# The sign of decoded float64 weights through a Prelu scaling, with the scaling back spread over three engines

## The chip, the cores and the metric

The kernel runs on one core of one Trainium2 chip. The metric is the device time of one execution in microseconds (us), as the median of several runs. Engines go by the profile's names: PE (TensorE matmul), PEld (its weight loads), DVE (VectorE), ACT (ScalarE), POOL (GpSimd), SP (the queue that issues the DMAs).

## The reference, cut to what matters

```python
# q, k, v: (8, 8, 576, 64); chunks of 64 along the sequence
attn = softmax((q_c @ k_c.T) / 8)            # per chunk
x = (attn @ v_c)  ->  (4608 tokens, 512)
h = x @ moe_w_in                             # 512 -> 2048
x = (h * sigmoid(h)) @ moe_w_out             # 2048 -> 512
h = x @ moe2_w_in                            # 512 -> 1024
s = h * softmax(h)
ln = (s - mean(s)) / sqrt(var(s) + 1e-6) * g_ln
out = ln @ moe2_w_out                        # 1024 -> 512
```

The four weight matrices reach the chip as float64, that is, as pairs of 32-bit words; the kernel makes float16 pairs (a high half and a low half that carry the value together) from them on the chip.

## The kernel before

The 4608 tokens are worked on in NB = 9 blocks of 512. For each block the kernel does the attention of four tiles of 128 tokens (`a_scores`, `a_norm`, `a_pv`; block 0 has a simpler form, `f_scores`, `f_norm`, `f_pv`), then the first layer in 16 groups (`h_group`, line 362 and on: twelve matmuls into one bank of PSUM, a Silu on ACT at L366, and `g_split`), then `x_part` (L645 to 647), which gives the input of the second MoE, and, one block later, that second MoE (`m_h`, `m_norm`, `m_out`). Blocks 0 and 1 (FAST = 2) use plain products; blocks 2 to 8 use a scheme with seven products in place of eight, whose combined weights are made during block 1 by `w1_sums` and `w2_sums` (L391 to L406) and written to DRAM.

Every value that enters a matmul is split by `split`: the high half is a float16 copy (L110 on ACT), the low half the value minus the high half (L114 on POOL, L115 on DVE).

**The decoding.** `wq` lists 48 tiles of weights, 128 x 512 float64 each: tiles 0 to 15 for w1, 16 to 31 for w2, 32 to 39 for w3 (names `w3q`), 40 to 47 for w4. `fetch` (L856 in the profile) starts the transfer of one into `wst`, a tile of pairs of int32 words. Three steps follow.

- `dec_scale` (`d1`): L129, ACT takes the upper word as a float32 and multiplies it by 2^-111, which brings the exponent into place. For tiles 0 to 31 the result is in PSUM (`wp`), for 32 to 47 in SBUF (`wy`).
- `dec_bits` (`d2`): three operations on DVE: L136 shifts left by 3, L137 takes in the top three bits of the lower word, and L139 takes the sign out of the upper word and puts it into bit 31.
- `dec_split` (`d3`): tiles 0 to 39 have the high half on ACT (L110) and the low half on POOL (L114); tiles 40 to 47 have their gain (`gs`, from g_ln) taken in, and the low half on DVE (L115).

`weights(n)` does the split of the oldest tile, the scaling of the next, and the bits of the one between; the lists NW0, NX, NW1 and NX1 say how often it is called at each step of blocks 0 and 1. The order on each engine is made by a scheduler from this program order with priorities (`tc.high_priority`); each engine then takes its instructions strictly in that order. The decoded value `wy` lives in tiles of the pools: from tile 28 on (`ytile`) all of them share two buffers (tag "o"), so that the scaling of a tile there needs the release by POOL, or DVE, of the tile two before it.

Attention tiles after block 0 have this chain: maximum (L215), difference (L224), Exp on ACT (L225) or in eight pieces (L222), sum (L226), factors (L231, L233), normalisation (L234, two SBUF operands on DVE), high half (L236 or a DVE copy), low half (L237, on POOL during block 0), a transposing DMA (pT, L239), and the matmuls with v (L256 to L258), whose halves vbh and vbl are made by `prep_v`.

Of the kernel before, what the change touches and what calls it, by code (L numbers as in the profile page):

```python
# [8 lines left out]
F32 = mybir.dt.float32  # L9
F16 = mybir.dt.float16  # L10
I32 = mybir.dt.int32
AF = mybir.ActivationFunctionType
ALU = mybir.AluOpType
# [3 lines left out]
P = 128  # L17
# [8 lines left out]
KD = DM // P  # L26
# [13 lines left out]
S_X2 = 2.0 ** 12  # L40
S_LN = 2.0 ** 10

LEAST = -3.4028234663852886e38


@with_exitstack
def fused(ctx: ExitStack, tc: tile.TileContext, qkv, w1, w2, w3, w4, g_ln, out):
    nc = tc.nc
    V, A, G, T = nc.vector, nc.scalar, nc.gpsimd, nc.tensor
# [19 lines left out]
    PHA = [4, 5, 6, 7, 8, 10, 11, 15, 32, 33, 34, 35]  # L69
    QF = 14  # L70
    DEFER = 7

    const = ctx.enter_context(tc.tile_pool(name="const", bufs=1))
    one = ctx.enter_context(tc.tile_pool(name="one", bufs=1))
# [9 lines left out]
    for d in range(KD):  # L84
        for f in range(4):
            if f % 2 == 0:
                tag = f"w2_{2 * d + f // 2}" if d < 3 else f"q{12 + f // 2}"
                y = one.tile([P, 2, 2, 4, P], F16, tag=tag, name="w2t")
# [8 lines left out]
    gs = const.tile([P, K2], F32, name="gs")  # L97
    mhalf = const.tile([P, 1], F32, name="mhalf")
    zero = const.tile([P, 1], F32, name="zero")


    qb = [const.tile([P, NS, P], F16, name=n) for n in ("qbh", "qbl")]
# [4 lines left out]
    def split(dst_h, dst_l, src, scale, eng_h, eng_l):  # L107

        if eng_h is A:
            A.activation(dst_h, src, AF.Copy, scale=scale)  # L110
        else:
            V.tensor_scalar(out=dst_h, in0=src, scalar1=scale, scalar2=None, op0=ALU.mult)
        if eng_l is G and scale == 1.0:
            return G.tensor_tensor(out=dst_l, in0=src, in1=dst_h, op=ALU.subtract).ins  # L114
        return V.scalar_tensor_tensor(out=dst_l, in0=src, scalar=scale, in1=dst_h,  # L115
                                      op0=ALU.mult, op1=ALU.subtract).ins
# [7 lines left out]
    def dec_scale(c):  # L124
        st, y, wh, wl, gain = c
        if c[1] is None:
            c[1] = ps1.tile([P, 512], I32, tag="mm", name="wp")
        p = c[1]
        A.activation(p.bitcast(F32), st[:, :, 1].bitcast(F32), AF.Copy, scale=2.0 ** -111)  # L129

    def dec_bits(c, y):
        st, p, wh, wl, gain = c
        c[1] = y
        if y is None:
            c[1] = y = p
        V.tensor_scalar(out=p, in0=p, scalar1=3, scalar2=None, op0=ALU.logical_shift_left)  # L136
        V.scalar_tensor_tensor(out=p, in0=st[:, :, 0], scalar=29, in1=p,  # L137
                               op0=ALU.logical_shift_right, op1=ALU.bitwise_or)
        V.scalar_tensor_tensor(out=y, in0=st[:, :, 1], scalar=-2 ** 31, in1=p,  # L139
                               op0=ALU.bitwise_and, op1=ALU.bitwise_or)  # L140

    def dec_split(c):
        st, y, wh, wl, gain = c
        yf = y.bitcast(F32)
        if len(wh.shape) == 3:
            yf = yf.rearrange("p (a b) -> p a b", a=wh.shape[1])
        if gain is None:
            split(wh, wl, yf, 1.0, A, G)
        else:
            split(wh, wl, yf, gain, A, V)  # L150


    ns = [0]
# [215 lines left out]
    def g_split(b, f, eng_h=V):  # L369
        return split(*g_of(b, f), graw.pop(f), S_G, eng_h, V)  # L370
# [318 lines left out]
    def m_fast(b, c, alt=False):  # L689
# [29 lines left out]
        def add(n, out, p, own=True):  # L719
# [3 lines left out]
                out=out, in0=p, in1=out if own else zero.to_broadcast([P, 512]), scale=1.0,  # L723
                scalar=LEAST if first else part[:, i:i + 1], op0=ALU.add, op1=ALU.max,
                accum_out=(part if first else m)[:, i:i + 1])
# [9 lines left out]
        elif not more_(b):  # L735
            uT_tags = ["q10", "q11"]
        m_norm(b, [2 * c, 2 * c + 1], [[(e[i], slice(0, F2))] for i in range(2)], m, e, u_tags, uT_tags,
               G if alt else UL, DEFER if c and more_(b) else 0)

# [90 lines left out]
    warm = const.tile([P, 1], F32, name="warm")  # L830
    G.memset(mhalf, -0.5)
    G.memset(zero, 0.0)
    ident = one.tile([P, P], F32, tag="h2", name="ident")
    make_identity(nc, ident)
    ident16 = const.tile([P, P], F16, name="ident16")
# [7 lines left out]
    for k in range(KD):  # L843
        for n in range(2):
            y = w3q[n, k // 2]
# [23 lines left out]
    def d1():  # L869
        if raw:  # L870
            i, st = raw.pop(0)
            c = [st, None if i < SB else ytile(i), *wq[i][1:]]
            dec_scale(c)
            mid.append((i, c))

    def d2():
        if mid:
            i, c = mid.pop(0)
            dec_bits(c, ytile(i) if i < SB else None)
            out_.append((i, c))  # L880
            if at[0] < 36 or len(raw) + len(mid) < 2:
                fetch()

    def d3():
        if out_:
            i, c = out_.pop(0)
            dec_split(c)

    def weights(n=1):
        for _ in range(n):  # L890
            d3()
            d1()
            d2()

    for x in FIRST:
# [6 lines left out]
        else:  # L902
            t = len(vs0)
            vs0.append(one.tile([P, 512], F32, tag=("vs", "xb0", "xb1", "xb2")[t], name=f"vs0_{t}"))
            nc.sync.dma_start(out=vs0[t], in_=qkv[t, :, 2])
    nc.sync.dma_start(out=gs, in_=g_ln)


    def first(i, what):
# [8 lines left out]
    for x in START.split():  # L918
        if x[0] in "snp":
            first(int(x[1]), x[0])  # L920
        else:
            {"d1": d1, "d2": d2, "d3": d3, "w": weights}[x]()
# [7 lines left out]
    for b in range(NB):  # L930
# [4 lines left out]
        for f in range(K1):  # L935
            if b < FAST:
# [10 lines left out]
                else:  # L947
                    y = g_split(b, f, A)
# [71 lines left out]
    b = NB - 1  # L1020
# [52 lines left out]
```

## Time and profile before

| what | value |
|---|---|
| median of 3 runs | 1180.05 us |
| the runs | 1181.21, 1178.99, 1180.05 us |
| span of the profiled execution | 1179.4 us |
| its own time outside the profile | not recorded apart; the span is 0.65 us below the median |
| PE busy | 1127.8 us (96%) |
| DVE busy | 911.7 us (77%) |
| ACT busy | 802.8 us (68%) |
| POOL busy | 249.1 us (21%) |
| chain that ended last | PE 59%, DVE 16%, ACT 10%, DMA 7%, issue 6%, POOL 2% |

Busy times count instructions that run; an engine that waits is idle. The chain is the work that ended last, followed back from the end of the span. The granted clock is the share of TensorE's full speed in a stretch. Names in rows are written as output<-inputs with buffer numbers left out, and a line can be that of a helper (L110, L114 and L115 stand for every split).

### The profile page before, as it was taken

To read this page: it belongs to the slowest core of one execution; us is meant where nothing else is said; L and a number is where in the kernel's file an instruction comes from. 1 tells how busy PE (TensorE), PEld (TensorE's weight loads), DVE (VectorE), ACT (ScalarE), POOL (GpSimd) and SP (SyncE) were. 2 spreads that over 40 slices of the span, in tenths; PEclk is the share of its full clock that TensorE was granted. 3 is DMA by queue.
4 is the path that set the end of the run, shared out by engine and by line. 5 is a ranking of instruction groups with operands and counts; after the bars stand their busy time and mean duration, and the time that the engine had idled before them with its cause. 6 is when DMAs were issued, how large, how long until landed. Compare 5 with 4: busy or idle time off the path is not lost.

```text
span 1179.4 us, 23566 instructions
## 1 busy us (share of the span) xinstructions
PE 1127.8 (96%) x9036; PEld 769.1 (65%) x9036; DVE 911.7 (77%) x1638; ACT 802.8 (68%) x1475; POOL 249.1 (21%) x243
## 2 busy tenths in 40 slices
PE   5999998998999999999999999999999999999998
PEld 4444443444657875887678767876787677777853
DVE  5999998487578787888778877888689868886453
ACT  6886678676667777856785677568756876577253
POOL 3655433334101510021003100310031002100001
PEclk9999899999999999999999999999999999999999
DMA  7667488543536564776577657666776676665704
GB/s 259 225 190 206 155 233 268 165 135 112 139 113 203 165 189 133 204 204 202 143 192 213 196 151 188 204 198 155 182 211 198 161 180 197 179 161 137 210 21 116
DMA packets 205169, 209.18 MB, mean 177 GB/s; under 512 B 120192, under 2 KB 130432, under 8 KB 205056
## 3 DMA queue, kind: packets, MB, share of 16 engines
q1 hardware_dynamic: 205056, 207.68, 61.5%
q8 instruction: 70, 1.15, 0.4%
q14 instruction: 43, 0.35, 0.1%
HBM read 156.24 MB, written 24.12 MB: 153 GB/s over the span
## 4 chain that ended last, share of the span: by engine, by line
PE 59%; DVE 16%; ACT 10%; DMA 7%; issue 6%; POOL 2%; SPq 0%; ACTq 0%; POOLq 0%; DVEq 0%
PE o_ps L821 5%; PE o_ps L813 5%; PE o_ps L814 5%; PE pa L491 3%; PE pa L594 3%; PE pa L592 3%; PE pa L593 3%; PE pa L493 3%; PE pa L492 3%; DVE vbl L115 2%; PE pa L708 2%; PE pa L709 2%; PE pa L710 2%; PE pb L491 2%; PE pb L493 2%
## 5 line engine op out<-in xcount | busy, mean ns | idle before, releaser
L110 ACT ACTIVATE q<-hc 128x512 f16<-128x512 f32 x196 | 119.1, 624 | 41.4 <-DVE hc L579 16.4
L115 DVE SCALAR_TENSOR_TENSOR q<-hc,q 128x512 f16<-128x512 f32 x196 | 138.0, 719 | 6.9 <-ACT q L110 5.5
L114 POOL TENSOR_TENSOR qbl<-qk,qbh 64x512 f16<-64x512 f32 x54 | 71.0, 1314 | 266.2 <-ACT qbh L110 223.6
L593 PE MATMUL pa<-q,ring 128*128 128x256 f16 x448 | 122.1, 273 | 0.0
L592 PE MATMUL pa<-q,ring 128*128 128x256 f16 x448 | 122.1, 273 | 0.0
L594 PE MATMUL pa<-q,ring 128*128 128x256 f16 x448 | 122.1, 273 | 0.0
L813 PE MATMUL o_ps<-w4h,uT 128*128 128x512 f16 x288 | 109.1, 379 | 0.4 <-DVE e L766 0.4
L814 PE MATMUL o_ps<-w4l,uT 128*128 128x512 f16 x288 | 109.2, 379 | 0.0
L779 POOL TENSOR_TENSOR c<-c,mhalf 128x2 f32<-128x2 f32 (+1 forms) x22 | 14.1, 640 | 392.1 <-DVE c L778 382.2
L492 PEld LDWEIGHTS <-ring 128*128 128x128 f16 x784 | 77.0, 98 | 18.4 <-issue 7.9
L491 PEld LDWEIGHTS <-ring 128*128 128x128 f16 x784 | 77.0, 98 | 11.5 <-DMA ring<-w1s 0.8
L592 PEld LDWEIGHTS <-ring 128*128 128x128 f16 x784 | 76.7, 98 | 11.1
L593 PEld LDWEIGHTS <-ring 128*128 128x128 f16 x784 | 76.7, 98 | 11.0
L493 PEld LDWEIGHTS <-ring 128*128 128x128 f16 x784 | 77.0, 98 | 9.2
L594 PEld LDWEIGHTS <-ring 128*128 128x128 f16 x784 | 76.7, 98 | 8.9
L821 PE MATMUL o_ps<-w4h,uT 128*128 128x512 f16 x288 | 70.2, 379 | 0.0
L491 PE MATMUL pa<-x,ring 128*128 128x256 f16 x224 | 61.6, 275 | 6.7 <-ACT hc L513 4.3
L493 PE MATMUL pa<-x,ring 128*128 128x256 f16 x224 | 61.7, 275 | 0.0
L492 PE MATMUL pa<-x,ring 128*128 128x256 f16 x224 | 61.6, 275 | 0.0
L491 PE MATMUL pb<-x,ring 128*128 128x256 f16 x224 | 61.1, 273 | 0.6 <-DMA ring<-w1s 0.6
L592 PE MATMUL pb<-q,ring 128*128 128x256 f16 x224 | 61.1, 273 | 0.0
L593 PE MATMUL pb<-q,ring 128*128 128x256 f16 x224 | 61.1, 273 | 0.0
(277 smaller groups left out, 3486.4 us busy)
## 6 DMA issues: line engine op xcount, KB each, us to landing
ring<-w1s SPq DMA_DIRECT2D x196, 256.0 KB, 3.4
ring<-w2s SPq DMA_DIRECT2D x196, 256.0 KB, 3.8
wst<-w SPq DMA_DIRECT2D x48, 512.0 KB, 4.1
qk<-qkv SPq DMA_DIRECT2D x29, 512.0 KB, 3.8
vs<-qkv SPq DMA_DIRECT2D x36, 256.0 KB, 3.2
out<-o SPq DMA_DIRECT2D x36, 256.0 KB, 2.2
w1s<-ws SPq DMA_DIRECT2D x32, 128.0 KB, 2.1
w2s<-ws SPq DMA_DIRECT2D x16, 256.0 KB, 2.0
```

What stands on the lines that cost most here:

```text
L110: A.activation(dst_h, src, AF.Copy, scale=scale)
L114: return G.tensor_tensor(out=dst_l, in0=src, in1=dst_h, op=ALU.subtract).ins
L115: return V.scalar_tensor_tensor(out=dst_l, in0=src, scalar=scale, in1=dst_h, op0=ALU.mult, op1=ALU.subtract).ins
L491: T.matmul(ps[:, c], wh, x[:, 0, k], start=first, stop=False, skip_group_check=True)
L492: T.matmul(ps[:, c], wh, x[:, 1, k], start=False, stop=False, skip_group_check=True)
L493: T.matmul(ps[:, c], wl, x[:, 0, k], start=False, stop=k == 1, skip_group_check=True)
L592: T.matmul(ps[:, c], wh, g[:, 0], start=first, stop=False, skip_group_check=True)
L593: T.matmul(ps[:, c], wh, g[:, 1], start=False, stop=False, skip_group_check=True)
L594: T.matmul(ps[:, c], wl, g[:, 0], start=False, stop=q == 1 and f == 3, skip_group_check=True)
L813: T.matmul(ps, uh[:, k], w4h[:, k, :], start=k == 0, stop=False)
L814: T.matmul(ps, uh[:, k], w4l[:, k, :], start=False, stop=False)
L821: T.matmul(ps, ul[:, k], w4h[:, k, :], start=False, stop=k == K2 - 1)
```

## The change

The scaling becomes a Prelu with scale 2^-108 and alpha -2^32: a positive value is multiplied by 2^-108, a negative one by 2^-108 and by -2^32, which makes it positive and sets the bit that the shift by 3 carries into bit 31, the sign. The third bit operation is left out, and the second one now writes `wy`. The decoded value is 2^24 times the weight, so it must be scaled by S_D = 2^-24. For tiles 0 to 39 the string WAYS says who does it: V (13 tiles), DVE subtracts with the scaling in one instruction; G (18 tiles), POOL multiplies by a broadcast constant and then subtracts; A (9 tiles), ACT scales in place and the split is as before. In ways V and G the high half takes the scaling in its own copy. For tiles 40 to 47, `gs` is scaled once on POOL.

```diff
+S_D = 2.0 ** -24
...
+    WAYS = "VG" * 8 + "GAV" * 5 + "G" + "AG" * 4
...
+    down = const.tile([P, 1], F32, name="down")
...
-        A.activation(p.bitcast(F32), st[:, :, 1].bitcast(F32), AF.Copy, scale=2.0 ** -111)
+        A.activation(p.bitcast(F32), st[:, :, 1].bitcast(F32), AF.Prelu, scale=2.0 ** -108, alpha=-2.0 ** 32)
...
         V.tensor_scalar(out=p, in0=p, scalar1=3, scalar2=None, op0=ALU.logical_shift_left)
-        V.scalar_tensor_tensor(out=p, in0=st[:, :, 0], scalar=29, in1=p,
+        V.scalar_tensor_tensor(out=y, in0=st[:, :, 0], scalar=29, in1=p,
                                op0=ALU.logical_shift_right, op1=ALU.bitwise_or)
-        V.scalar_tensor_tensor(out=y, in0=st[:, :, 1], scalar=-2 ** 31, in1=p,
-                               op0=ALU.bitwise_and, op1=ALU.bitwise_or)
-
-    def dec_split(c):
+
+    def dec_split(c, i):
...
-        if gain is None:
-            split(wh, wl, yf, 1.0, A, G)
+        if gain is not None:
+            return split(wh, wl, yf, gain, A, V)
+        way = WAYS[i]
+        if way == "A":
+            A.activation(yf, yf, AF.Copy, scale=S_D)
+            return split(wh, wl, yf, 1.0, A, G)
+        A.activation(wh, yf, AF.Copy, scale=S_D)
+        if way == "G":
+            G.tensor_tensor(out=yf, in0=yf, in1=down.to_broadcast([P, 512]).rearrange("p (a b) -> p a b", a=KD)
+                            if len(yf.shape) == 3 else down.to_broadcast([P, 512]), op=ALU.mult)
+            G.tensor_tensor(out=wl, in0=yf, in1=wh, op=ALU.subtract)
         else:
-            split(wh, wl, yf, gain, A, V)
+            V.scalar_tensor_tensor(out=wl, in0=yf, scalar=S_D, in1=wh, op0=ALU.mult, op1=ALU.subtract)
...
+    G.memset(down, S_D)
...
+    G.tensor_scalar(out=gs, in0=gs, scalar1=S_D, scalar2=None, op0=ALU.mult)
```

The lines of the changed kernel: Prelu L133; shift L140; second bit operation L141; A: scaling L153, then L114 and L118 as before's L110 and L114; G and V: high half L155; G: L157 and L159 on POOL; V: L161 on DVE. Before's L110, L114 and L115 are L114, L118 and L119 there, and later lines are 11 higher (L226 is L237, L234 is L245, L406 is L417).

The scheduler also places the remaining instructions differently. PE's order is the same. Three places:

DVE in block 0, at the normalisation of attention tile 4, the first of block 1 (`ae`; `as` its sums, `g` a split of the first layer). Before:

```order
L139 SCALAR_TENSOR_TENSOR wy_934<-wst_778,wp_835 128x512
L136 TENSOR_SCALAR wp_932<-wp_932 128x512
L136 TENSOR_SCALAR wp_942<-wp_942 128x512
L137 SCALAR_TENSOR_TENSOR wp_932<-wst_821,wp_932 128x512
L226 TENSOR_REDUCE as_909<-ae_908 128x8
L139 SCALAR_TENSOR_TENSOR wy_944<-wst_821,wp_932 128x512
L231 TENSOR_SCALAR as_909<-as_909 128x8
L137 SCALAR_TENSOR_TENSOR wp_942<-wst_831,wp_942 128x512
L233 RECIPROCAL ar_923<-as_909 128x8
L139 SCALAR_TENSOR_TENSOR wy_1034<-wst_831,wp_942 128x512
L234 TENSOR_TENSOR ae_908<-ae_908,ar_923 128x512
```

In the changed kernel (its L226, L235, L237, L245 are before's L215, L224, L226, L234):

```order
L226 TENSOR_REDUCE am_899<-s_ps_874 128x8
L140 TENSOR_SCALAR wp_926<-wp_926 128x512
L119 SCALAR_TENSOR_TENSOR g_852<-h_ps_838,g_852 128x512
L235 TENSOR_TENSOR ae_901<-s_ps_874,am_899 128x512
L141 SCALAR_TENSOR_TENSOR wy_938<-wst_815,wp_926 128x512
L140 TENSOR_SCALAR wp_936<-wp_936 128x512
L141 SCALAR_TENSOR_TENSOR wy_1027<-wst_825,wp_936 128x512
L237 TENSOR_REDUCE as_902<-ae_901 128x8
L242 TENSOR_SCALAR as_902<-as_902 128x8
L244 RECIPROCAL ar_916<-as_902 128x8
L161 SCALAR_TENSOR_TENSOR w2t_90<-wy_938,w2t_90 128x512
L245 TENSOR_TENSOR ae_901<-ae_901,ar_916 128x512
```

Between the sum and the normalisation stood two L139 and one L137; now one L161 stands there.

ACT near the end of block 0, ahead of `vbh`, the high half of v for one of the attention tiles of block 1 (w2t_95 are the last two tiles of w2; `wy`<-`wst` is the scaling of a tile of w3; x2_2 belongs to `x_part`). Before:

```order
L110 ACTIVATE w2t_94<-wy_1368 128x512
L129 ACTIVATE wp_1376<-wst_1221 128x512
L129 ACTIVATE wy_1386<-wst_1362 128x512
L110 ACTIVATE w2t_95<-wy_1378 128x512
L110 ACTIVATE w2t_95<-wy_1388 128x512
L110 ACTIVATE x2_2_1432<-x2_ps_1329 128x512
L110 ACTIVATE vbh_115<-vs_1325 64x8x64 x2
L110 ACTIVATE x_1179<-x_ps_1435 128x4x128
L129 ACTIVATE wy_1396<-wst_1372 128x512
```

In the changed kernel:

```order
L114 ACTIVATE w2t_94<-wy_1359 128x512
L155 ACTIVATE w2t_95<-wy_1369 128x512
L133 ACTIVATE wy_1376<-wst_1352 128x512
L155 ACTIVATE w2t_95<-wy_1378 128x512
L153 ACTIVATE wy_1376<-wy_1376 128x512
L114 ACTIVATE w3q_104<-wy_1376 128x512
L114 ACTIVATE x2_2_1421<-x2_ps_1320 128x512
L133 ACTIVATE wy_1386<-wst_1362 128x512
L114 ACTIVATE vbh_116<-vs_1316 64x8x64 x2
L114 ACTIVATE x_1170<-x_ps_1424 128x4x128
L133 ACTIVATE wy_1393<-wst_1372 128x512
```

The scaling and the high half of the first tile of w3 (wy 1376, L153 and L114) and the scaling of the second (L133, wy 1386) have come to stand before `vbh`.

DVE in block 1, at the last tile of w4 (`w4l`; `c`, `mp`, `e`, `u` belong to the norm of the second MoE); the split of `g` and the lines L403 to L406 of `w1_sums` follow on both sides. Before:

```order
L137 SCALAR_TENSOR_TENSOR wy_2041<-wst_1984,wy_2041 128x512
L139 SCALAR_TENSOR_TENSOR wy_2041<-wst_1984,wy_2041 128x512
L778 SCALAR_TENSOR_TENSOR c_1949<-dv_1946,c_1949 128x1
L670 TENSOR_REDUCE mp_2073<-h2_ps_2046 128x1
L782 TENSOR_SCALAR e_1925<-e_1925,nmu_1944,c_1949 128x1024
L115 SCALAR_TENSOR_TENSOR g_2036<-g_2034,g_2036 128x512
L670 TENSOR_REDUCE mp_2073<-h2_ps_2047 128x1
L115 SCALAR_TENSOR_TENSOR w4l_109<-wy_1979,gs_110,w4h_108 128x512
L784 TENSOR_TENSOR u_1931<-e_1925,u_1931 128x1024
L672 TENSOR_REDUCE mm__2076<-mp_2073 128x1
L115 SCALAR_TENSOR_TENSOR w4l_109<-wy_2041,gs_110,w4h_108 128x512
```

In the changed kernel:

```order
L780 TENSOR_SCALAR nmu_1929<-us_1927 128x1
L789 SCALAR_TENSOR_TENSOR c_1934<-dv_1931,c_1934 128x1
L681 TENSOR_REDUCE mp_2056<-h2_ps_2029 128x1
L793 TENSOR_SCALAR e_1910<-e_1910,nmu_1929,c_1934 128x1024
L119 SCALAR_TENSOR_TENSOR g_2020<-g_2018,g_2020 128x512
L681 TENSOR_REDUCE mp_2056<-h2_ps_2030 128x1
L795 TENSOR_TENSOR u_1916<-e_1910,u_1916 128x1024
L683 TENSOR_REDUCE mm__2059<-mp_2056 128x1
L772 TENSOR_SCALAR nm_2062<-mm__2059 128x1
L119 SCALAR_TENSOR_TENSOR g_2020<-g_2103,g_2020 128x512
```

The two bit operations and both `w4l` of before have left this piece for earlier places.

## Rows read from the trace of the kernel before

**Rows 1.** The page, part 1: busy time of each engine over the whole span.
```profile
PE 1127.8 (96%) x9036; PEld 769.1 (65%) x9036; DVE 911.7 (77%) x1638; ACT 802.8 (68%) x1475; POOL 249.1 (21%) x243
```

**Rows 2.** Busy time by stretch: start:end, length, engines, granted clock, DMA share, GB/s.
```profile
29.50:72.70 43.20, 43.06 (x192) 19.08 (x192) 39.50 (x63) 36.73 (x66) 24.73 (x22) 0.96 0.65 215
72.70:131.20 58.50, 52.53 (x386) 26.15 (x385) 53.63 (x89) 42.67 (x98) 32.39 (x27) 0.91 0.64 192
131.20:197.70 66.50, 60.01 (x294) 28.59 (x293) 62.86 (x115) 53.15 (x95) 24.42 (x24) 1.00 0.77 225
...
94.30:97.70 3.40, 3.40 (x15) 1.24 (x11) 3.23 (x6) 1.67 (x3) 3.39 (x4) 0.50 0.68 214
121.60:128.40 6.80, 6.20 (x36) 3.01 (x37) 6.60 (x9) 3.48 (x6) 2.48 (x2) 0.50 0.60 196
```

**Rows 3.** Waits of PE, 70 to 215 us: total, times, longest, in us.
```profile
PE x_ps L256 <- ACT vbh L110: 2.1, 1, 2.1
PE h_ps L362 <- DVE y L406: 2.1, 1, 2.1
PE x_ps L256 <- DMA pT<-ae: 2.1, 1, 2.1
PE x_ps L258 <- DVE vbl L115: 0.9, 2, 0.6
PE x_ps L645 <- DVE g L115: 0.8, 1, 0.8
PE h_ps L362 <- ACT g L366: 0.8, 1, 0.8
```

**Rows 4.** Groups by line and shape, 0 to 215 us: busy us, mean ns.
```profile
L139 DVE SCALAR_TENSOR_TENSOR wy<-wst,wp 128x512 int32<-128x512 int32 x32 | 21.5, 680 | 1.4 <-POOL w2t L114 1.0
...
L129 ACT ACTIVATE wp<-wst 128x512 f32<-128x512 f32 x32 | 20.3, 637 | 4.4 <-DMA wst<-w 4.3
L114 POOL TENSOR_TENSOR w2t<-wy,w2t 128x512 f16<-128x512 f32 x16 | 19.4, 1215 | 17.5 <-ACT w2t L110 12.1 <-DMA vs<-qkv 5.4
...
L139 DVE SCALAR_TENSOR_TENSOR wy<-wst,wy 128x512 int32<-128x512 int32 x16 | 14.5, 904 | 0.3
...
L129 ACT ACTIVATE wy<-wst 128x512 f32<-128x512 f32 x16 | 10.8, 677 | 11.3 <-POOL w3q L114 6.7 <-DVE w4l L115 3.1 <-POOL w2t L114 1.4
L114 POOL TENSOR_TENSOR w3q<-wy,w3q 128x512 f16<-128x512 f32 x8 | 10.3, 1288 | 15.2 <-ACT w3q L110 15.2
...
L115 DVE SCALAR_TENSOR_TENSOR w4l<-wy,gs,w4h 128x512 f16<-128x512 f32 x8 | 7.4, 933 | 0.0
...
L110 ACT ACTIVATE w3q<-wy 128x512 f16<-128x512 f32 x8 | 5.0, 620 | 1.2 <-DVE wy L139 1.2
```

**Rows 5.** DVE in order of time, 81 to 93 us: start, duration, in us.
```profile
82.53 0.68 DVE L139 SCALAR_TENSOR_TENSOR wy<-wst,wp 128x512 int32<-128x512 int32 x1
...
84.38 0.69 DVE L139 SCALAR_TENSOR_TENSOR wy<-wst,wp 128x512 int32<-128x512 int32 x1
84.99 0.68 DVE L234 TENSOR_TENSOR ae<-ae,ar 128x512 f32<-128x512 f32 x1
...
91.76 1.57 DVE L234 TENSOR_TENSOR ae<-ae,ar 128x512 f32<-128x512 f32 x1
```

**Rows 6.** POOL in order of time, 88 to 94 us.
```profile
88.04 1.15 POOL L237 TENSOR_TENSOR ae<-ae 128x512 f16<-128x512 f32 x1
...
91.62 2.73 POOL L114 TENSOR_TENSOR w2t<-wy,w2t 128x512 f16<-128x512 f32 x2 [1.19 <-ACT w2t L110]
```

**Rows 7.** ACT in order of time, 115 to 122 us; in brackets idle and releaser.
```profile
115.64 0.67 ACT L129 ACTIVATE wy<-wst 128x512 f32<-128x512 f32 x1 [1.39 <-POOL w2t L114]
...
119.29 0.63 ACT L110 ACTIVATE w2t<-wy 128x512 f16<-128x512 f32 x1 [2.46 <-DVE wy L139]
...
120.30 1.27 ACT L110 ACTIVATE vbh<-vs 64x512 f16<-64x512 f32 x2
```

**Rows 8.** DVE in order of time, 182 to 195 us.
```profile
182.75 1.16 DVE L139 SCALAR_TENSOR_TENSOR wy<-wst,wy 128x512 int32<-128x512 int32 x1
...
194.27 0.42 DVE L406 TENSOR_TENSOR y<-wq,y 128x256 f32<-128x256 f32 x1
```

More of the change, by code (lines that the diff above doesn't have):

```diff
@@ L886, in d3 @@
             i, c = out_.pop(0)
-            dec_split(c)
+            dec_split(c, i)
     def weights(n=1):
```

## Prediction

> **What bounds the kernel now.** I read the page's first part, then the stretches, then who waits for whom on PE, then single places in order of time. PE is busy 1127.8 of 1179.4 us [rows 1], so the most that can be had is the 51.6 us in which it is not, and what a lowered clock costs. The changed instructions all lie in the first 200 us, where weights are decoded beside the work on blocks 0 and 1. There the stretches [rows 2] say three things. From 29.5 to 72.7 us PE is full (43.06 of 43.20): faster decoding gains nothing there but a lead. From 72.7 to 131.2 us PE is idle for 5.97 of 58.5 us while DVE is busy for 53.63 (92%) and POOL for 32.39 (55%): DVE is the crowded engine. From 131.2 to 197.7 us PE is idle for 6.5 us and DVE is at 62.86 of 66.5 (95%). Inside the middle stretch two pieces have TensorE at a granted clock of 0.50, its 1.2 GHz level: 3.4 us after a PE stretch of waiting, and 6.8 us after another. At 2.4 GHz the same columns take half: 1.7 and 3.4 us are lost there.
>
> PE's own waits [rows 3] name the places: a wait for g (0.8), for the transposed pT of tile 4 (2.1), twice for vbl (0.9, the longer 0.6), for vbh (2.1), for a g of ACT (0.8), and for y from L406 (2.1). All hang on DVE, or on ACT and POOL behind DVE.
>
> **The change part by part.** *The third bit operation goes.* 32 instructions of 680 ns and 16 of 904 ns [rows 4]: 32 x 0.680 + 16 x 0.904 = 36.2 us less on DVE. The second bit operation now writes wy itself; it has the operands of the removed one, so I take the removed one's 680 ns against no row of its own, a difference of nothing.
>
> *Prelu for Copy* on ACT: the same 128x512 float32 scaling, 637 and 677 ns now [rows 4]. Prelu is in no row of before; the nearest are these and the 620 ns of another ACT copy. I take no change; 0.05 us either way on 48 tiles is 2.4 us of an engine that is 73% busy in the middle stretch (42.67 of 58.5 [rows 2]). The order of ACT holds as many table loads as before, 41, so no load is priced.
>
> *The scaling back by three engines.* By the string of ways, 13 tiles go to DVE, 18 to POOL with two operations, 9 to ACT with one more copy. (a) DVE: 13 new instructions with two SBUF operands. The nearest row is the low half of w4, 933 ns; without company such a shape takes 0.68 us and beside POOL 1.57 [rows 4, 5]. At 0.9: 11.7 us; ends 8.8 and 20.4. DVE's net is 36.2 - 11.7 = 24.5 us less, ends 15.8 and 27.4. (b) POOL: 18 multiplies of 128x512 come, 13 subtracts go to DVE. The nearest rows are its subtracts of 1215 and 1288 ns, and 1.36 in a pair beside DVE [rows 4, 6]; at 1.25 that is 22.5 - 16.3 = 6.2 us more; with 0.68 (the same work on DVE) it is -4, with 1.36 it is +8. POOL has 26 us free in the middle stretch, so its busy time costs nothing; its latency does: a tile of way G is ready 1.25 us later. (c) ACT: 9 copies at 0.62 [rows 4], 5.6 us, hidden as long as nothing that PE needs stands behind them. The scaling of gs and one memset run once on POOL at the start: nothing, 0.3 us at the worst.
>
> Now the places, in PE's order, as what each does to the end time.
> 1. Wait for g, 0.8 [rows 3]: DVE is 91% busy before it [rows 2] and loses 0.68 us per tile. Gone: **-0.8** (ends 0 and -0.8).
> 2. Wait for pT of tile 4, 2.1 [rows 3]. The chain before it: two third bit operations stand between the tile's sum and its normalisation at 84.99 [rows 5], and POOL starts the low half only at 88.04 [rows 6]. In the new order one decoding operation (the new L161) stands between the two in place of three (L139, L137, L139), which is 2 x 0.68 = 1.4 us, and the earlier L139s are gone too, so the low half ends earlier by more than the wait. Gone: **-2.1** (ends 0 and -2.1). The 3.4 us at half clock that follow it [rows 2] I take as gone with the wait: **-1.7** (ends 0 and -1.7). But PE then reaches the next tile's pT sooner, whose own normalisation took 1.57 beside POOL [rows 5]: **+1.0** (ends 0 and 2.1, the wait that it replaces).
> 3. Wait for vbl: **-0.5** (of 0.9).
> 4. Wait for vbh at about 120 us. ACT now has three more rows ahead of vbh: the scaling of tile 32 (0.62), its high half (0.62), and the Prelu of tile 33 (0.68), which needs one of the two buffers of wy and so POOL's release; such a wait took 1.39 [rows 7]. Together 3.3 us, of which 2.4 fit into the 2.46 that ACT idled there for L139 [rows 7]: **+0.9** (ends 0 and +3.3). I leave the 6.8 us of half clock behind it where they are.
> 5. Wait for g from ACT at 161 us, 0.8: ACT came late through two waits on the decode of w4, which is now shorter by 0.904 a tile: **-0.8** (ends 0 and -0.8).
> 6. Wait for L406 at 194.27, 2.1 [rows 3, 8]. Ahead of it on DVE stood the last tile's L137 and L139 (1.16 for the latter alone) and its w4l; in the new order they have left this place altogether. Gone: **-2.1** (ends 0 and -2.1).
> 7. Five of the 13 new DVE instructions lie in the middle stretch; each may meet POOL at 1.57 - 0.68 = 0.89: at most 4.5 us, of which I take **+0.5**, since a DVE with 24.5 us less to do has gaps for the rest.
>
> Sum: -0.8 - 2.1 - 1.7 + 1.0 - 0.5 + 0.9 - 0.8 - 2.1 + 0.5 = -5.6 us against the span of 1179.4. That span stands 0.65 below the median of 1180.05, so on the scale of the median: 1180.05 - 5.6 = 1174.5. About 0.2% (2.4 us) is what a measurement of this kernel can tell from no change.
>
> The row on point 7 shows what company costs: the normalisation took 1.57 at 91.76, while POOL was in the subtract that began at 91.62, and 0.68 at 84.99 [rows 5, 6]. The Trainium skill, SBUF — State Buffer, section "Who interferes with whom", says that a DVE instruction with two SBUF inputs contends with a GpSimd instruction that reads SBUF, and that the later one blocks fully. By that rule the change trades 32 removed operations that took one operand from PSUM, and disturbed nobody, for 13 that contend, against a POOL with more to do; the trace agrees at this place, and what follows from it is rival A.
>
> **The rivals.** *A. Collisions eat DVE's gain in the middle stretch.* Operand pairs in SBUF beside POOL take 1.57 [rows 5], and POOL's pair took 2.73 for two there [rows 6]. If all five new DVE instructions of the middle stretch meet POOL, and all on the chain that PE waits for, 5 x 0.89 = 4.5 us come back, of which the sum holds 0.5: +4.0. For it: POOL at 55% and rising. Against: POOL's idle 26 us, and that eight of the 13 lie before 72 us, under a full PE. Time: 1174.5 + 4.0 = 1178.5, no change.
>
> *B. Slower: ACT is held at the two buffers of wy.* ACT takes its work in order. Its scalings of tiles 31 to 39 already waited 8.1 us for POOL in eight rows (6.7 + 1.4 [rows 4]), and behind them stand vbh, x and the Silu. If each of the five G tiles there (31, 33, 35, 37, 39) holds the ring for one more POOL operation, that is 5 x 1.29 = 6.4 us, and the four A tiles add 4 x 0.62 = 2.5: 8.9 us on ACT's queue. It decides if more than 5.6 of that reaches PE. For it: the new order puts a Prelu directly before vbh. Against: the same tiles lose 0.904 us of DVE each, and most waits lie where PE has other work. If all lands: -5.6 + 8.9 = +3.3, so 1183.3.
>
> *C. More: the 6.8 us at half clock vanish too.* If PE does not wait for vbh, nothing breaks its work ahead of 121.6 us; half of 6.8 is 3.4 us [rows 2]: 1171.1. For it: PE's stop there is one wait of 2.1. Against: point 4 lengthens it.
>
> **How the numbers follow.** The forecast, 1174.5, has 0.55; its own range, from the ends of points 2, 4 and 6, is 1172 to 1177. C has 0.16, A 0.17, B 0.12, since B needs most of its price to land. Faster by over 0.2%: 0.55 + 0.16 = 0.71; within: A, 0.17; slower: B, 0.12. The range takes in C with 2 us to spare and A whole, and goes halfway into B's side: 1169 to 1181.
>
> **What would show it.** After the change DVE's busy time should be near 911.7 - 24.5 = 887, POOL's near 255, ACT's near 808. Right: PE's waits for g, pT of tile 4 and L406 are gone or under half, and no piece at half clock stands near 95 us. Wrong for point 4 or for B: PE's wait for vbh is over 3.5 us, or ACT's waits of Prelu on POOL sum to well over 8.1 us. Wrong for point 7 or for A: the new DVE instruction's mean is over 1.2 us. Prelu at over 0.75 us, or an idle PE between 131 and 198 us that stays above 6 us, would make the whole forecast too low.

## The result and the profile after

The changed kernel takes 1189.37 us (median of 4 runs, 1187.76 to 1191.84), the kernel before on the same chip 1179.52 us (4 runs, 1178.80 to 1181.21). The ratio is 1.0082, 95% interval 1.0062 to 1.0101: some 9.7 us slower, where 5.6 us faster was forecast. The span of the profiled execution went from 1179.4 to 1187.3 us.

The page's first part, to be held against [rows 1]:

```profile
PE 1130.5 (95%) x9036; PEld 769.7 (65%) x9036; DVE 894.6 (75%) x1603; ACT 807.4 (68%) x1484; POOL 254.7 (21%) x250
```

The load of the engines came out nearly as forecast: ACT 807.4 (808 was said), POOL 254.7 (255), DVE 894.6 (887). DVE has 17.1 us less to do (24.5 was said), and the kernel is slower. Stretches, columns as in [rows 2]; the last four are pieces at half clock, that is, at a granted clock of 0.50 (1.2 GHz):

```profile
72.70:131.20 58.50, 50.73 (x374) 25.33 (x371) 46.36 (x75) 44.63 (x102) 32.22 (x28) 0.91 0.62 182
131.20:197.70 66.50, 59.65 (x275) 27.60 (x274) 53.71 (x98) 49.54 (x88) 26.27 (x25) 0.95 0.75 214
101.10:107.90 6.80, 4.82 (x33) 2.63 (x34) 5.52 (x11) 3.41 (x6) 2.74 (x4) 0.50 0.80 210
...
165.90:169.30 3.40, 3.40 (x9) 1.15 (x8) 1.97 (x8) 3.37 (x8) 0.00 (x0) 0.51 1.05 306
186.40:189.80 3.40, 3.40 (x11) 1.38 (x10) 1.42 (x9) 3.39 (x7) 0.67 (x2) 0.51 1.02 383
278.60:285.40 6.80, 5.74 (x33) 2.82 (x34) 6.32 (x11) 2.15 (x4) 2.90 (x3) 0.50 0.48 163
```

DVE's share between 72.7 and 131.2 us fell from 92% to 79% (46.36 of 58.5), yet PE does less in the same time, 50.73 us in place of 52.53. After 90 us the half clock lasts for 27.3 us in all (six pieces, the one at the very end left out), before for 17.1 (four). Half of the difference, 5.1 us, is an estimate of what that costs; it is an upper one, since PE was not busy in all of it. All six pieces begin in a stop of PE or just behind one: the wait for pT ends at 103.1 us, and its piece runs from 101.1; the wait for a Silu ends at 165.5, and the clock falls at about 166. Such a stop costs twice. Not every stop does: one at 270 us in before (2.85 us, for a vbl) has no piece behind it, and the same stop in the changed kernel (3.08 us) has the 6.8 us at 278.6.

Waits of PE, as [rows 3]:

```profile
PE x_ps L267 <- DMA pT<-ae: 4.3, 1, 4.3
PE h_ps L373 <- ACT g L377: 3.9, 3, 3.0
PE wq L402 <- DVE y L417: 3.0, 1, 3.0
PE x_ps L267 <- DVE wy L141: 1.4, 1, 1.4
PE x_ps L267 <- ACT vbh L114: 1.1, 1, 1.1
```

The longest wait of before in this window is not among [rows 3]:

```profile
PE wq L391 <- DVE e L766: 2.9, 1, 2.9
```

The same matmul waits 3.0 us in the changed kernel, for y of L417; that stop is not new. The waits for g of DVE (0.8) and for y at 194 us (2.1) of [rows 3] are gone. The wait for pT of the first attention tile (2.1) has become one of 1.4 us for L141: by the kernel, x_ps takes a PSUM bank of the kind in which a tile of weights (wp) is held until L141 has read it. New are 4.3 us for pT, now of the second attention tile, and 3.0 in one piece for a Silu.

PE's order is the same in both kernels, so the start of each matmul can be compared with itself. The lead of the changed kernel is worked out from the two traces:

| place | before, us | after, us | behind (+) or ahead |
|---|---|---|---|
| x_part behind the first attention tile | 97.73 | 93.99 | -3.7 |
| second attention tile, waits for pT | 101.88 | 103.08 | +1.2 |
| after the half clock behind it | 105.04 | 108.05 | +3.0 |
| end of block 0 | 128.34 | 129.18 | +0.8 |
| matmul that waits for the Silu | 162.38 | 165.51 | +3.1 |
| after the half clock at 186 us | 183.40 | 189.59 | +6.2 |
| y of w1_sums, last tile of w4 in before | 194.75 | 198.80 | +4.1 |
| within block 2, half clock in after | 276.01 | 285.07 | +9.1 |
| end of the span | 1179.4 | 1187.3 | +7.9 |

Up to 98 us the gain is there. The table shows three losses: at the second attention tile, between 129 and 190 us, and 3 us at the half clock near 280 us. For the last, the trace shows no cause in the changed instructions, which all lie in the first 200 us. **At the second tile**, DVE, then POOL, then ACT in order of time:

```profile
81.53 1.03 DVE L242 TENSOR_SCALAR as<-as 128x8 f32<-128x8 f32 x1
...
82.71 1.36 DVE L161 SCALAR_TENSOR_TENSOR w2t<-wy,w2t 128x512 f16<-128x512 f32 x1
84.00 1.64 DVE L245 TENSOR_TENSOR ae<-ae,ar 128x512 f32<-128x512 f32 x1
86.86 0.70 DVE L140 TENSOR_SCALAR wp<-wp 128x512 int32<-128x512 int32 x1 [1.22 <-ACT wp L133]
```

```profile
82.49 1.04 POOL L157 TENSOR_TENSOR wy<-wy,down 128x512 f32<-128x512 f32 x1
83.60 1.48 POOL L159 TENSOR_TENSOR w2t<-wy,w2t 128x512 f16<-128x512 f32 x1
```

```profile
85.67 0.63 ACT L247 ACTIVATE ae<-ae 128x512 f16<-128x512 f32 x1 [3.34 <-DVE ae L245]
```

L161 takes 1.36 and the normalisation L245 1.64 beside POOL's pair L157 and L159 (alone, the normalisation took 0.68 [rows 5], and L161 has a median of 0.69 in its first eight tiles). Even L242, of 128x8 elements, takes 1.03; the POOL instruction beside it is a subtract of the attention (kb, 81.37 to 82.53), not one of the pair. ACT's next row is the high half L247, so it stands still for 3.34 us, the scalings behind it come late, and DVE in turn idles 1.22 for one of them. The second tile's maximum is behind that row, and its pT with it. By the end of block 0 most of the loss here is made good: 3.0 us behind at 108 us, 0.8 at 129 us. **In w3**, the chain of work that ended last goes through POOL twice per tile of way G:

```profile
125.78 0.64 ACT w3q L155
...
126.46 0.09 issue
126.55 1.17 POOL wy L157
127.71 0.07 issue
127.78 1.16 POOL w3q L159
...
128.97 0.68 ACT wy L133
```

From 125.78 to 128.97 ACT's L155, POOL's L157 and L159 and the next scaling follow each other with less than 0.15 us between them. From the first low half of w3 to the end of the last the trace shows 28.5 us (121.7 to 150.2); in the kernel before 23.2 (123.5 to 146.6).

### The profile page after: what moved, and what is told of

Read it like the earlier page. It is cut to its first block, busy times and chain, and to the rows that moved or that the text cites. A ratio compares the mean times of both kernels' runs of the same rounds, so it can differ in the third digit from the quotient of the medians.

```text
span 1187.3 us, 23540 instructions
## 1 busy us (share of the span) xinstructions
PE 1130.5 (95%) x9036; PEld 769.7 (65%) x9036; DVE 894.6 (75%) x1603; ACT 807.4 (68%) x1484; POOL 254.7 (21%) x250
## 4 chain that ended last, share of the span: by engine, by line
PE 52%; DVE 15%; ACT 9%; issue 6%; DMA 6%; POOL 3%; SPq 0%; POOLq 0%; ACTq 0%; DVEq 0%
PE o_ps L824 4%; PE o_ps L825 4%; PE o_ps L832 4%; PE pa L605 3%; PE pa L604 3%; PE pa L603 3%; PE pa L502 3%; PE pa L504 3%; PE pa L503 3%; DVE vbl L119 3%; DMA vs<-qkv 2%; PE pa L721 2%; PE pa L719 2%; PE pa L720 2%; ACT u L783 2%
## 5 line engine op out<-in xcount | busy, mean ns | idle before, releaser
L114 ACT ACTIVATE q<-hc 128x512 f16<-128x512 f32 x196 | 119.1, 624 | 41.6 <-DVE hc L590 16.3
L119 DVE SCALAR_TENSOR_TENSOR q<-hc,q 128x512 f16<-128x512 f32 x196 | 137.8, 718 | 6.9 <-ACT q L114 5.5
L118 POOL TENSOR_TENSOR qbl<-qk,qbh 64x512 f16<-64x512 f32 x54 | 71.1, 1317 | 268.5 <-ACT qbh L114 216.7
L502 PE MATMUL pa<-x,ring 128*128 128x256 f16 x224 | 61.0, 272 | 7.3 <-ACT hc L524 5.0
L605 PE MATMUL pb<-q,ring 128*128 128x256 f16 x224 | 61.1, 273 | 0.0
L603 PE MATMUL pb<-q,ring 128*128 128x256 f16 x224 | 61.1, 273 | 0.0
L604 PE MATMUL pb<-q,ring 128*128 128x256 f16 x224 | 61.1, 273 | 0.0
L502 PE MATMUL pa<-xb,ring 128*128 128x256 f16 x224 | 61.1, 273 | 0.0
```

What stands on the lines that cost most here:

```text
L502: T.matmul(ps[:, c], wh, x[:, 0, k], start=first, stop=False, skip_group_check=True)
L603: T.matmul(ps[:, c], wh, g[:, 0], start=first, stop=False, skip_group_check=True)
L604: T.matmul(ps[:, c], wh, g[:, 1], start=False, stop=False, skip_group_check=True)
L605: T.matmul(ps[:, c], wl, g[:, 0], start=False, stop=q == 1 and f == 3, skip_group_check=True)
```

## The experiments

Theory 1: DVE and POOL disturb each other at the two-operand instructions. Theory 2: whatever relieves DVE makes the scheduler draw an order that loses what it wins. Ratios are to the kernel before on the same chip; "us" worked out from them take 1180 as a whole. The tiles are numbered as in `wq`, and e1 to e18 are the runs.

**e1_prelu_alone.** The sign through Prelu needs no other scale: the scale of before, 2^-111, works with alpha -2^32, and then nothing has to be scaled back.

The third bit operation is left out, and `dec_split` stays as before.

```diff
-        A.activation(p.bitcast(F32), st[:, :, 1].bitcast(F32), AF.Copy, scale=2.0 ** -111)
+        A.activation(p.bitcast(F32), st[:, :, 1].bitcast(F32), AF.Prelu, scale=2.0 ** -111, alpha=-2.0 ** 32)
...
-        V.scalar_tensor_tensor(out=p, in0=st[:, :, 0], scalar=29, in1=p,
+        V.scalar_tensor_tensor(out=y, in0=st[:, :, 0], scalar=29, in1=p,
                                op0=ALU.logical_shift_right, op1=ALU.bitwise_or)
-        V.scalar_tensor_tensor(out=y, in0=st[:, :, 1], scalar=-2 ** 31, in1=p,
-                               op0=ALU.bitwise_and, op1=ALU.bitwise_or)
```

> Edit on the kernel before: Prelu with scale 2^-111 (not 2^-108) and alpha -2^32, the third bit operation left out; the value then has the scale that it had before, so nothing is scaled back and no engine gets an operation more. Theory 1 (company): the loss of the change comes from the operations that scale back, POOL's pairs above all, which hold up DVE at the attention chain of tile 4. It expects a gain here, 1172 to 1177 us, and no wait of PE for pT over 2 us between 95 and 110 us. Theory 2 (order): with DVE relieved the scheduler draws another order on ACT, and this order makes the second attention tile late whatever is added. It expects 1184 us or more and a wait for pT near 4 us.

1179.47 us, ratio 0.9995 (0.9984 to 1.0005). No gain: theory 1's number falls, and theory 2's too (no 4 us wait for pT, not 1184). The relief of DVE is worth 0.6 us here, within the interval nothing, so the loss of the change, 10.3 us against e1, comes with the scaling back. The lead of 5.0 us at 93 us is gone at 122 us, behind two waits for vbl (2.0 and 1.6) and this one of PE between them:

```profile
PE x_ps L254 <- ACT vbh L110: 4.3, 1, 4.3
```

**e2, e3: the changed kernel with ways replaced in tiles 16 to 31.** e2: G by A; e3: V by A.

> Edit on the changed kernel: in tiles 16 to 31 every way G is A (string VG x 8, AAV x 5, A, AG x 4): POOL has no pairs there, ACT six copies more. Theory 1 expects the normalisation L245 of tile 4 back at 0.7 us, the wait for pT of the second tile under 2 us, and 1181 to 1184 us in all. Theory 2 expects no more than 1.5 us of difference to the changed kernel, 1187 to 1191 us.

> Edit on the changed kernel: in tiles 16 to 31 every way V is A (string VG x 8, GAA x 5, G, AG x 4): DVE has no scaling subtract there, POOL keeps its six pairs. Theory 1 in the form that DVE's new two-operand instructions are the cause expects 1181 to 1184 us; in the form that POOL's pairs are, no gain, 1187 to 1191 us. Theory 2 expects 1187 to 1191 us too.

e2: 1188.93, ratio 1.0071 (1.0051 to 1.0091), with a wait for pT of 4.2 and L245 still at 1.65, now beside a single subtract of POOL. e3: 1194.19, 1.0119 (1.0094 to 1.0144). The wait for pT is gone there, but PE stops for as long at the same tile, 1.5 us for vbh and 2.7 for vbl. So theory 1 falls in both forms, while neither run takes the stop at the second tile away. e2 says something of the clock too: in its trace the half clock after 90 us lasts 17.1 us, as long as in before, and it is 8.4 us slower, so the clock alone is not the loss.

**e4_pairs_on_before.**

> Edit on the kernel before: the third bit operation stays, Copy stays; in the 18 tiles that have way G in the changed kernel POOL multiplies by 1.0 first and then subtracts. Theory 1 expects the price of the pairs alone: 1184 to 1190 us. Theory 2 expects little, 1178 to 1182 us, since DVE is not relieved and the order stays near that of before.

1194.10, ratio 1.0116 (1.0098 to 1.0134): 13.7 us for 18 multiplies by one, and an order drawn anew with them. Theory 2's number falls; POOL's second operation is dear. Theory 3: the round trip of the two buffers of wy.

**e5, e6, e7: four buffers for tiles 28 to 39** (tags h4 to h7 in place of o), on before, on the change and on e1; **e8:** no pairs in w3.

```diff
+        elif i < 40:
+            pool, tag = one, ("h4", "h5", "h6", "h7")[i % 4]
         else:
             pool, tag = two, "o"
```

> Edit on the kernel before: tiles 28 to 39 take wy from four buffers (tags h4 to h7, idle at that time) in place of the two of tag o. Theory 3 (ring): what holds ACT, and with it vbh and the Silu behind the decoding, is the round trip of two buffers (scaling on ACT, bits on DVE, high half on ACT, low half on POOL, release), not the amount of work on DVE. It expects a gain of its own, 1172 to 1177 us, and ACT's waits of L129 for POOL, 8.1 us before, under 3 us. Theory 2 (any redrawn order loses what it wins) expects 1178 to 1183 us.

> The same four buffers in the changed kernel. Theory 3 expects that most of the loss goes, since POOL's pair then no longer stands in the round trip: 1178 to 1183 us. Theory 1 (company of DVE and POOL) expects a small change, 1186 to 1190 us, since the collisions stay.

> The Prelu at 2^-111 without a third bit operation and without scaling back, with the four buffers. Theory 3 expects that DVE's 36 us show up once the ring is out of the way: 1166 to 1174 us. Theory 2 expects 1177 to 1182 us.

> Edit on the changed kernel: tiles 32 to 39 all go way A (string VG x 8, GAV x 5, G, A x 8), so POOL has no pair in the two-buffer ring. Theory 3 expects a gain over the changed kernel by shorter round trips in w3, about 4 tiles x 0.5 us each: 1185 to 1188 us. Theory 1 expects 1187 to 1191 us.

e5: 1182.66, 1.0013 (1.0004 to 1.0023); ACT's scalings wait for POOL 0.8 us in place of 8.1, as theory 3 said, and nothing is gained. e6: 1189.50, 1.0072 (1.0052 to 1.0093). e7: 1178.19, 0.9975 (0.9965 to 0.9985). e8: 1184.39, 1.0033 (1.0020 to 1.0047). Of the times, only e8's is as theory 3 said, and a little better; e5 and e7 are within what theory 2 said. e8 also shows what the second tile is worth: it has the same stop there (4.4 us, and 6.8 us of half clock), yet in its trace it is 0.6 us ahead of before at the end of block 0 and 1.0 behind at the matmul that waits for the Silu, where the changed kernel is 3.1 behind. In e6 the decoding of w3 lasts for 19.5 us in place of 28.5 and the time stays; PE there waits 3.9 for pT and 2.8 for x, and the half clock after 90 us is 20.5 us. The number of buffers alone is not the cause.

**e9, e10, e11: one way at a time on e1.** POOL's multiply (by one) in the 18 tiles of way G; DVE's low half in the 13 of way V; ACT's extra copy in the 9 of way A. **e12:** the changed kernel without both places, that is, tile 21 goes way A in place of V (its subtract stands ahead of L245), and tiles 32 to 39 all go way A.

> On the kernel of e1 (Prelu at 2^-111, nothing to scale back), POOL multiplies by 1.0 ahead of its subtract in the 18 tiles of way G alone; all others as in e1. Theory 4 (two places): what the change lost against e1, about 10 us, comes mostly from POOL's second operation where it lengthens the round trip of w3, and less from DVE's subtract ahead of the normalisation of tile 4. It expects 1184 to 1188 us. Theory 5 (any addition to the decoding costs the same, since three engines take turns on one tile) expects 1182 to 1184 us.

> On the kernel of e1, the low half of the 13 tiles of way V is made by DVE in place of POOL, and nothing else. Theory 4 expects 1181 to 1184 us, with PE waiting over 2 us for pT of the second attention tile. Theory 5 expects 1178 to 1181 us, since no operation is added, one is moved from a slower engine to a faster.

> On the kernel of e1, ACT copies the value in place once more in the 9 tiles of way A, and nothing else. Theory 4 expects 1179 to 1182 us. Theory 5 expects 1182 to 1184 us, as for way G per operation.

> On the changed kernel, the tile whose DVE subtract stands ahead of the normalisation of attention tile 4 (tile 21) goes way A, and tiles 32 to 39 go way A (string VG x 8, GAVGAAGAVGAVGAVG, A x 8). Theory 4 expects both losses gone: 1178 to 1182 us, no wait for pT of the second tile over 2 us. Theory 5 expects the value of e8, 1183 to 1186 us.

| part | ratio | 95% interval | us over e1 |
|---|---|---|---|
| e1: relief of DVE | 0.9995 | 0.9984 to 1.0005 | - |
| e9: way G, 1188.24 us | 1.0061 | 1.0042 to 1.0079 | +7.8 |
| e10: way V, 1181.20 us | 1.0001 | 0.9986 to 1.0015 | +0.7 |
| e11: way A, 1182.92 us | 1.0012 | 0.9997 to 1.0026 | +2.0 |
| sum with e1's -0.6 | | | +9.9 over before |
| the change itself | 1.0082 | 1.0062 to 1.0101 | +9.7 over before |

The parts add up to the whole, but the sum is known to some 4 us only: e10 and e11 are not apart from e1 by their intervals, and e1 stands in it three times. Nor need parts add: the 18 multiplies cost 13.7 us on before (e4) and 7.8 on e1 (e9). The part that is clear of noise is way G. (The times are medians; the traces of e9 and e10 are of executions 3 to 4 us faster, those of e1, e2 and e12 of executions 2 to 4 us slower.) e12 is at 1183.84 (1.0020, 1.0007 to 1.0033), not apart from e8. It does not settle the second tile, since the stop there stayed in its trace:

```profile
PE x_ps L267 <- DVE as L237: 3.8, 1, 3.8
```

Way G came out 0.2 us above what theory 4 said and 4 above theory 5's range; e11 and e12 lie in theory 5's ranges, and e10 between the two. So what is shown is the price of way G, not that of the second tile.

**e13 and e14: the round trip of w3 lengthened and shortened on e1.**

> On the kernel of e1, POOL multiplies by 1.0 first in tiles 33, 35, 37 and 39 alone (the four of way G in w3), nothing else. Theory 6 (the price of POOL's second operation lies where the tile's round trip is what ACT waits for, in w3): 4 to 7 us over e1's 1179.5, so 1183 to 1187 us. Rival 7 (each of the 18 pairs costs its share, 7.8 / 18 = 0.43 us): 1180.5 to 1182 us.

> On the kernel of e1, DVE makes the low half in tiles 28 to 39 in place of POOL (0.68 us in place of 1.16 and one engine fewer in the round trip). Theory 6 expects the opposite of e13, a gain of 2 to 5 us over e1: 1174.5 to 1178 us, with ACT's waits of the scaling for a release under 4 us (7.5 in e1). Rival 7 expects 1178.5 to 1181 us.

e13: 1184.94, ratio 1.0052 (1.0037 to 1.0067): four multiplies cost 6.7 us over e1; the 14 others share the rest of the 7.8. This is the one run in which the order is all but held: laid beside e1's, ACT and DVE have one row each in another place, PE none, POOL the four multiplies (and one memset at the start), and SP a few transfers, from 133 us on. So the price of these four is not that of another order. e14: 1176.97, 0.9981 (0.9969 to 0.9993), 1.7 under e1, not apart from it by the intervals; ACT's scalings wait 2.3 us for a release there, by DVE (under 4 was said), and 3.3 for loads. Theory 6 holds for the price; the gain that it said is not shown. ACT's waits, 100 to 170 us, of e1:

```profile
ACT wy L129 <- POOL w3q L114: 5.4, 5, 1.8
...
ACT wy L129 <- POOL w2t L114: 2.1, 2, 1.4
```

and of e13:

```profile
ACT wy L131 <- POOL w3q L151: 8.1, 4, 3.2
...
ACT wy L131 <- POOL w3q L116: 3.1, 2, 1.7
...
ACT wy L131 <- POOL w2t L116: 2.1, 2, 1.4
```

7.5 us have become 13.3, and POOL's last low half of w3 ends at 142.2 in place of 137.8. Of PE's waits the one for y of w1_sums grew most; of e1, then of e13:

```profile
PE h_ps L662 <- DVE y L404: 2.0, 1, 2.0
```

```profile
PE h_ps L674 <- DVE y L416: 4.2, 2, 2.2
```

In order of time, POOL of e13 (first and last tile of w3, and one pair beside DVE):

```profile
113.84 1.16 POOL L116 TENSOR_TENSOR w3q<-wy,w3q 128x512 f16<-128x512 f32 x1
...
131.15 2.14 POOL L149 TENSOR_TENSOR wy<-wy,down 128x512 f32<-128x512 f32 x1 [1.90 <-ACT w3q L148]
133.37 1.49 POOL L151 TENSOR_TENSOR w3q<-wy,w3q 128x512 f16<-128x512 f32 x1
...
140.73 1.49 POOL L151 TENSOR_TENSOR w3q<-wy,w3q 128x512 f16<-128x512 f32 x1
```

A pair stands for 3.7 us there at the worst (131.15 to 134.86).

**e15 to e18: what DVE's relief is worth, and the best version.** e15 and its control e17 change one list, `NX = [2, 3, 2, 3, 0, 3, 1, 2]`; e16 is e14 with four buffers; e18 is e16 with this list.

> On the kernel of e1, NX = [2, 3, 2, 3, 0, 3, 1, 2] in place of [2, 3, 2, 1, 0, 6, 0, 2]: three of the six tiles decoded in one step ahead of the last attention tile of block 1 are decoded elsewhere. If e1's gain of 4.5 us at 97 us is lost because ACT has this burst ahead of vbh (theory 8), PE's wait for vbh there falls from 4.3 to under 2.5 us and the time to 1175 to 1178 us. If what holds vbh is the chain of loads and matmuls of v itself (rival 9), the wait stays over 3.5 us and the time within 1178 to 1182 us.

> e14 with the four buffers of e7 for tiles 28 to 39. If the round trip is what counts, the two edits do the same thing twice: 1173 to 1178 us, close to the better of e7 and e14. If release and latency are separate costs, the gains add: 1171 to 1174 us.

> Control of e15: the kernel before (Copy, third bit operation) with the same NX = [2, 3, 2, 3, 0, 3, 1, 2]. If the spreading is what gained the 5 us of e15, this gains 3 to 6 us over before. If the 36 us less on DVE gained them, once the decoding was spread, it gains under 1.5 us.

> The version that the runs point to: Prelu at 2^-111 without scaling back, low halves of tiles 28 to 39 on DVE, four buffers for their values, and the spread NX of e15. If the gains of e15 and e16 have different places: 1168 to 1172 us at a before of 1179 to 1180. If both shorten the same wait: 1172 to 1176 us.

e15: 1173.72, ratio 0.9960 (0.9948 to 0.9973). e17: 1185.31, 1.0050 (1.0037 to 1.0063). The same list costs 5.9 us with the third bit operation and gains 4.1 without it over e1: the relief is worth 10.6 us under this list and 0.6 under the other. PE's wait for vbh in e15:

```profile
PE x_ps L254 <- ACT vbh L110: 3.5, 1, 3.5
```

At 3.5 it lies between what theories 8 and 9 named, so the burst ahead of vbh is not shown as the place. e16: 1175.25, 0.9964 (0.9951 to 0.9978). e18: 1174.56, 0.9957 (0.9944 to 0.9970), the same within the intervals: the gains of e15 and e16 do not add. In the traces of e16 and e18 the half clock after 90 us lasts 6.8 us, in before 17.1, so up to 5 us of their gain is clock, by the same estimate. In e18 DVE makes the first two and the last low half of w3 thus:

```profile
114.17 1.29 DVE L117 SCALAR_TENSOR_TENSOR w3q<-wy,w3q 128x512 f16<-128x512 f32 x2 [0.37 <-ACT w3q L112]
...
128.50 0.69 DVE L117 SCALAR_TENSOR_TENSOR w3q<-wy,w3q 128x512 f16<-128x512 f32 x1
```

and PE's wait for vbh is

```profile
PE x_ps L266 <- ACT vbh L112: 1.4, 1, 1.4
```

w3 takes 15.0 us from 114.2 to 129.2. e15, e16 and e18 all beat both kernels, by 0.36 to 0.43% of before.

## Why the prediction was wrong, by its steps

- **Prices of single operations held.** The rows of the changed kernel:

```profile
L157 POOL TENSOR_TENSOR wy<-wy,down 128x512 f32<-128x512 f32 x18 | 19.5, 1084 | 32.8 <-ACT w L155 14.4 <-ACT w2t L155 10.9 <-ACT w3q L155 7.4
...
L133 ACT ACTIVATE wy<-wst 128x512 f32<-128x512 f32 x16 | 10.7, 675 | 11.6 <-POOL w3q L159 5.9 <-DVE w4l L119 2.0 <-DMA wst<-w 1.7
...
L161 DVE SCALAR_TENSOR_TENSOR w<-wy,w 128x512 f16<-128x512 f32 x8 | 6.9, 862 | 1.3 <-ACT w L155 1.2
...
L161 DVE SCALAR_TENSOR_TENSOR w2t<-wy,w2t 128x512 f16<-128x512 f32 x5 | 4.7, 938 | 0.8 <-ACT w2t L155 0.7
```

  L161 was put at 0.9 (0.862 and 0.938), POOL's multiply at 1.25 (1.084), Prelu at no change (675 ns against 677). Rival A's test, L161 over 1.2, was not met, and e10 prices all of way V at 0.7 us, not apart from nothing. That a DVE instruction with two SBUF inputs contends with a GpSimd instruction that reads SBUF is what the Trainium skill says (SBUF — State Buffer, "Who interferes with whom"), and the trace agrees at the second tile, with 1.64 us for L245 against 0.68. The prediction counted the 32 removed operations that read PSUM; the 16 others (904 ns [rows 4]) had both inputs in SBUF, so the change also took company away.
- **Points 1 and 6 held, point 2's first half in part:** 3.7 us ahead at 98 us (4.6 said), and 2.1 us won at the y of w1_sums. The half clock near 95 us is gone, but the stop ahead of it went from 2.1 to 1.4 us only, since another release, that of L141, ended next.
- **Point 2's second half, +1.0, failed:** the wait for the next pT was 4.3 us and brought 6.8 us of half clock. The table of leads and e8 show that most of this is made good by 129 us, behind the waits for v of the third tile.
- **Point 4** had the wrong sign: the wait for vbh was to grow by 0.9 and fell from 2.1 to 1.1, since PE came to it later. As the place of rival B it was wrong too.
- **The step that failed is (b), "its busy time costs nothing; its latency does", with no term for that latency in the sum.** A tile of way G was said to be ready 1.25 us later, and nothing was charged. The four of w3 cost 6.7 us with the order all but held (e13), and without them the change is 5.8 us faster (e8); all 18 cost 7.8 (e9), the nine copies of ACT 2.0 (e11, within the noise), where nothing, or 0.9 at one place, was in the sum.
- **Point 5 failed:** it was to gain 0.8, and the wait became 3.0. w3 took 28.5 us in place of 23.2, but the trace does not show that this holds the Silu, since further on the decoding of w4 has caught up (the scaling of tile 44 starts at 156.92, in before at 156.84). The Silu, at 161.75 in before, starts at 164.87, behind the scaling of tile 46, which in before stands behind it (175.77):

```profile
164.31 0.66 ACT L133 ACTIVATE wy<-wst 128x512 f32<-128x512 f32 x1 [1.70 <-DMA wst<-w]
164.87 0.59 ACT L377 ACTIVATE g<-h_ps 128x512 f32<-128x512 f32 x1
```

  That scaling waited for its load, and the load for its turn. L141 had left the buffer at 156.99, but SP issues its transfers in order, and three stores of combined weights, which waited for POOL's low halves of them, stood first:

```profile
157.55 2.31 SPq L428 DMA_DIRECT2D w1s<-ws  x3
159.91 0.42 SPq L422 DMA_DIRECT2D w1s<-w  x1
160.43 0.93 SPq L868 DMA_DIRECT2D wst<-w  x2
```

  So this part of the loss is one of order, on ACT and on SP; how much of the 9.7 us it is, no run tells.
- **The gain was overrated too.** Named waits were counted as gone for good; e1, with all of the relief and none of the price, gained 0.6 us. What PE won by 93 us it gave back at the waits for vbl and vbh by 122 us.
- **Rival B had the side and, in part, the mechanism** (ACT held in w3 for one more POOL operation per tile), with a chance of 0.12. Its five G tiles at 6.4 us are near the 6.7 of e13's four, and its 8.9 us in all near the 10.3 by which the change stands above e1. Its time, 1183.3, was too low, since it kept the whole gain of 5.6. Its sign, ACT's waits for POOL well over 8.1, is met in e13 (13.3) and not in the changed kernel itself, where they are 7.8; only the single wait is longer, 5.9 in four at the pairs, 6.7 in seven in before. Of the other signs of being wrong one was met: PE idles for 6.85 us between 131 and 198 us, over the 6 that were named.

Open: the way from w3's longer decoding to PE in the changed kernel; why four buffers take ACT's waits away in e5 and 9 us off the decoding of w3 in e6, and nothing off the time; why e3, whose five tiles of way V become A, is 4.4 us slower than the change; and where e15 wins, since its wait for vbh stayed. What these have in common, that an order drawn anew moves stops of PE and half clock with them, was not tried apart: e13 alone holds the order. e15 and e17 show that one list moves the time by 4 to 6 us either way.

## What to carry to other kernels

Where three engines take turns on one tile and hand over a small ring of buffers, price an added operation by the round trip that it lengthens, at the tiles where an in-order engine waits for the release, and not by the free time of the engine that does it. Add it alone, to a kernel whose order it leaves as it is, to see the price. Relief of a crowded engine is worth what the next wait in line leaves of it: try the relief alone, under two orders, before paying for it. Before scaling a result back, ask for a constant that makes it unnecessary.

## What the runs showed of the hardware

POOL's multiply by a broadcast column took 1.04 us at the median, less than its subtract (1.16), and up to 2.14 beside DVE (e13). A DVE instruction on 128x8 elements (L242) took 1.03 us beside a subtract of POOL, and 0.17 at the median of its 32. SP issued a load 3.4 us after its buffer was free, behind stores that waited for POOL. Prelu with a slope of -2^32 took as long as a copy (631 and 675 ns against 637 and 677) and brought no table load (41 on both sides; ACT has nine instructions more in all, the nine copies of way A).
